# Delta-rule attention and a routed expert layer on one core: keys and queries laid out with rows of zeros between the heads and loaded in one transfer per half turn

## The chip, the cores and the metric

The kernel runs on one core of a Trainium2 chip. The metric is the device time of one execution in microseconds (us). Engines are named as in the profile: PE (TensorE, with its weight loads as PEld), DVE (VectorE), ACT (ScalarE), POOL (GpSimd) and SP (SyncE, which only issues transfers).

## The reference

The first part is a delta rule over 768 steps, for 4 batches and 8 heads of 48 features. Its output, as 3072 rows of 384, goes to one of 8 experts each:

```python
k_n = k / (np.linalg.norm(k, axis=-1, keepdims=True) + 1e-06)
for t in range(S):                                    # S = 768
    kt, vt, bt = (k_n[:, :, t], v[:, :, t], beta[:, :, t, None])
    y[:, :, t] = np.einsum('bhd,bhde->bhe', q[:, :, t], state)
    v_old = np.einsum('bhde,bhd->bhe', state, kt)
    state = state + bt[:, :, :, None] * np.einsum('bhd,bhe->bhde', kt, vt - v_old)
...
logits = x @ w_gate                                   # x: (3072, 384), 8 experts
expert_idx = np.argmax(logits, axis=1)
gate_w = softmax(logits) at expert_idx
for e in range(E):
    y[rows of e] = np.maximum(x[rows of e] @ w1[e], 0.0) @ w2[e]      # F = 1024
return gate_w[:, None] * y
```

## The kernel before

The 768 steps are cut into 12 turns (`NT`) of 64 steps (`C`). The 32 pairs of batch and head are held as 16 slots with two heads each: head half e = 0 lies in partitions 0 to 47 and e = 1 in partitions 64 to 111 (`feat`, L298); partitions 48 to 63 between them belong to no head.

**Keys and queries.** `kqA` is a ring of 6 turns (`RING`), 2048 columns of fp32 for each: 1024 columns of keys (k = 0) and 1024 of queries (k = 1), with the features on partitions. `load_kq(t)` (L348) fills one turn with four transfers of 48 partitions by 1024 columns (192 KB), one for each half turn k and head half e. All are issued by SP, but for the e = 1 keys of turns 0 and 1, which ACT issues. The matrix multiplications with the state, `with_state` (L548), contract over partitions 0 to 111, so partitions 48 to 63 of a slot must hold zeros. They come from memsets on POOL for slots 2 to 5 (L332) and slot 0 (L1086), and for slot 1 from two transfers that copy 16 partitions of slot 5 (L336). `kS` (L560) makes each use of the state wait for the zeroing too.

**A turn.** `scores(t)` (L363) multiplies the keys with the keys and queries of the turn on PE. From turn 2 on it does so in two halves through one pair of banks (BY), and ACT evicts each half with two activations (L309, into `blkA` and `pA`) before the next half can start. `invert(n)` (L418) serves two turns: DVE gets the norms `nt` (L472) and then a triangular inverse of 32 by 32 blocks, whose transposed result `TT` (L517) the two turns use. For n = 0 the diagonal blocks come straight from PSUM (L311 and L309); for later n four small transfers copy them from SBUF to SBUF (`blkA<-blkA`). DVE also masks the query-key scores of each turn (L412). `load_kv(t)` (L521) loads the values `v` and the keys by token `kt`; ACT scales the 16 slots of v by the norms (L530, 16 activations). `turn(t)` (L563) is the recurrence: ACT puts v into PSUM, PE adds the state's part (L554), ACT evicts the residual R, PE applies the inverse (L583), ACT evicts Z, PE goes across the two 32-blocks (L593), then R, the inverse and Z once more, and `kz` (L607) with ACT's copies S gives the next state. `output` (L623) writes the turn's rows to `xs`, `logits` and `route` choose the experts, and `early` and `expert` run the experts' two matrix multiplications (L945, L977). `last_rows` (L910) writes 1.18 MB of zeros into the tail of `xs` from the tile `folds`.

**What sets the order.** Every step is recorded with `P.op`: engine, an assumed cost, what it reads and writes, a rank (`prio`) and an assumed latency of its result (`lat`). `Plan.order` (L88) plays these through and so decides in which order each engine gets its instructions; an engine then runs them in that order and waits where data is missing. The constants `cf` (masks, identity, numbers; 128 rows of 805 fp32) are one transfer issued by ACT (L319). Each load uses one of eight completion counters in turn: from the ninth on, the built program issues a load only after the one eight before it is complete.

Of the kernel before, what the change touches and what calls it, by code (L numbers as in the profile page):

```python
# [18 lines left out]
B, H, S, D = 4, 8, 768, 48  # L19
C = 64  # L20
NT = S // C
FQ = 8
# [11 lines left out]
FAR = 1 << 20  # L34
RING = 6
AHEAD = 5
RUN = 4.5
PAGE, FILL, STALL = 125, 3.8, 0.8
OUT, LOG = 0.9, 0.2
# [153 lines left out]
def _consts():  # L193

    p = np.arange(128)[:, None]
    j = np.arange(128)[None, :]
    rev = np.broadcast_to(E - np.arange(E), (128, E))
    first = np.broadcast_to(np.arange(E), (128, E))  # L200
    closed = first + E * EARLY * (first == 0)
    i = np.arange(32)[None, :]
    q = np.arange(64)[None, :]
    parts = [
        ("rev", rev), ("first", first), ("upper", E * (p < j)), ("ones", np.full((128, 128), E)),
        ("ident", p == j), ("numbers", 128 * np.arange(2 * NT)[None, :] + p + 1), ("along", np.broadcast_to(j, (128, 128))),
        ("later", np.concatenate([p % 64 < q, (p % 64) ^ 32 < q], axis=1)), ("fold", p % 32 == i), ("sums", p % 64 == q),
        ("places", np.broadcast_to(E * (CAP + 128 * np.arange((NL - CAP) // 128)), (128, (NL - CAP) // 128))),
        ("closed", closed),
    ]  # L210
    at, where = 0, {}
    for name, a in parts:
        where[name] = (at, a.shape[1])
        at += a.shape[1]
    return np.concatenate([a for _, a in parts], axis=1).astype(np.float32), where
# [3 lines left out]
def tile_kernel(ctx: ExitStack, tc: tile.TileContext, kq, ktok, vtok, betal, wgk, w1, w2, out):  # L219
    nc = tc.nc  # L220
    P = Plan()
# [8 lines left out]
    fc, where = _consts()  # L230
    cf = pool.tile([128, fc.shape[1]], FP32, name="cf")
# [8 lines left out]
    bl = pool.tile([128, NB, 32], FP32, name="bl")  # L240
    cnt = pool.tile([128, E], FP32, name="cnt")
    kqA = pool.tile([128, RING * 2048], FP32, name="kqA")
    pA = pool.tile([128, RING * 1024], FP32, name="pA")
    blkA = pool.tile([128, 13 * 1024], FP32, name="blkA")
    kts = [pool.tile([128, 2 * FQ, D], FP32, name=f"kt{i}") for i in range(2)]

    vs = [pool.tile([128, FQ, 2, D], FP32, name=f"v{i}") for i in range(2)]
# [14 lines left out]
    def kb(b):  # L262
        return [("bk", b), ("bk", b + 1)]
# [3 lines left out]
        return kqA[:, a : a + 2048].rearrange("p (k s c) -> p k s c", k=2, c=C)  # L267

    def kKQ(t, ks=(0, 1)):
        return [("kqA", t % RING, k, e) for k in ks for e in range(2)]  # L270

    def Pm(t):
        a = (t % RING) * 1024
# [19 lines left out]
    SP = lambda b: max(0.5, b / 220e3)  # L293

    def dma(eng, o, i):
        return lambda: eng.dma_start(out=o, in_=i)

    def feat(e):  # L298
        return slice(64 * e, 64 * e + D)
# [16 lines left out]
    P.op("DVE", 0.1, lambda: nc.vector.memset(tiny[:], 0.0), w=["tiny"], prio=-99)  # L316
    P.op("ACT", 0.2, lambda: nc.scalar.activation(out=tiny[:], in_=tiny[:], func=AF.Copy), w=["tiny"], prio=-45)
    P.op("ACT", 0.5, dma(nc.scalar, bl[:], betal), w=["bl"], prio=-49, lat=2.5)
    P.op("ACT", 0.5, dma(nc.scalar, cf[:], nc.inline_tensor(fc, name="c_f32").ap()), w=["cf"], prio=-48, lat=8.5)  # L319
    P.op("DVE", 0.2, lambda: nc.vector.memset(wg[:], 0.0), w=["wg"], prio=-48)  # L320
    P.op("ACT", 0.5, dma(nc.scalar, wg[:, :, 0:E], wgk), w=["wg"], prio=-40, lat=2.5)
    P.op("DVE", 1.0, lambda: nc.vector.memset(pairs[0][:], 0.0), w=kb(BS), prio=-50)
# [4 lines left out]
        for e in range(2):  # L327
            nc.tensor.matmul(bk[BR + e], lhsT=zeros[:, 0:128], rhs=zeros[:], start=True, stop=True, skip_group_check=True)
    P.op("PE", 1.0, adding, r=["zeros"], w=kb(BR), prio=-95, passes=4, use=2048)

    for i in (2, 3, 4, 5):
        P.op("POOL", 1.85, lambda i=i: nc.gpsimd.memset(kqA[:, 2048 * i : 2048 * i + 2048], 0.0),  # L332
             w=kKQ(i) + [("zero", i)], prio=-60)
    for e in range(2):
        r = slice(64 * e + D, 64 * e + 64)
        P.op("SP", 0.6, dma(nc.sync, kqA[r, 2048:4096], kqA[r, 10240:12288]), r=[("zero", 5)], w=[("zero", 1)],  # L336
             prio=-40, lat=2.5)
    empty = pool.tile([128, E * NL // 128 * 2], FP32, name="empty")


# [7 lines left out]
    def load_kq(t):  # L348
        o = kqA[:, (t % RING) * 2048 : (t % RING) * 2048 + 2048]
        for k in range(2):  # L350
            for e in range(2):
                eng, q = (nc.scalar, "ACT") if t < 2 and e and not k else (nc.sync, "SP")
                c = slice(1024 * k, 1024 * k + 1024)
                P.op(q, 0.9, dma(eng, o[feat(e), c], kq[t, e][:, c]), w=[("kqA", t % RING, k, e)],
                     prio=(t - 100 if not k else t - 60) if t < 2 else t - 7, lat=4.4 if t < 2 and not k else 2.5)

    def products():
        for f in range(FQ):
# [4 lines left out]
    def scores(t):  # L363
# [35 lines left out]
        else:  # L399
            for g in range(2):  # L400
                P.op("PE", 1.1, lambda g=g: run(BY, (0, 1), range(4 * g, 4 * g + 4)), r=kKQ(t), w=kb(BY),
                     prio=t - RUN + 0.01 * g, passes=32, use=770)
                src = pairs[3][:].rearrange("p e (f c) -> p e f c", f=4)
# [3 lines left out]
                    src[:, :, :, 0:C].rearrange("p e f c -> p c e f")),  # L407
                    r=kb(BY), w=[("XY", n % 3, u, g)], prio=t - RUN)
                P.op("ACT", 0.5, copy("ACT", Pm(t)[:, :, 4 * g : 4 * g + 4, :], src[:, :, :, C:]),
                     r=kb(BY), w=[("P", t % RING)], prio=t - RUN)  # L410
        later = const("later").rearrange("p (e c) -> p e c", e=2).unsqueeze(2).to_broadcast([128, 2, FQ, C])
# [108 lines left out]


    def load_kv(t):
        P.op("SP", SP(393216), dma(nc.sync, vs[t % 2][:].rearrange("p f e d -> p (f e d)"), vtok[t]),
             w=[("v", t % 2)] + [("vn", t % 2, i) for i in range(2 * FQ)], prio=t - 3.5, lat=4.0 if t < 2 else None)
        P.op("SP", SP(393216), dma(nc.sync, kts[t % 2][:].rearrange("p f d -> p (f d)"), ktok[t]),
             w=[("kt", t % 2)], prio=t - 3.4, lat=4.0 if t < 2 else None)
        nt, u = nts[t // 2 % 3], t % 2
        for i in range(2 * FQ):
            v = vs[t % 2][:, i % FQ, i // FQ, :]
            P.op("ACT", 0.225, lambda v=v, i=i: nc.scalar.activation(  # L530
                out=v, in_=v, func=AF.Copy, scale=nt[:, 16 * u + i : 16 * u + i + 1]),
                r=[("nt", t // 2 % 3), ("v", t % 2)], w=[("vn", t % 2, i)], prio=t - VP)
# [25 lines left out]
                    )  # L558

    def kS(t):  # L560
        return [("S", t % 2, e) for e in range(2)] + [("zero", t % RING)]

    def turn(t):  # L563

# [485 lines left out]

    for i in range(NT + AHEAD + 1):
        t = i - AHEAD
        for m, g in enumerate(groups):
            if m >= CLOSE and g[-1] == 2 * t - 3:
                route(m, 1)
        if t > 0:
            output(t - 1)
            if 2 * t - 3 == groups[CLOSE][-1]:
                listed(range(CLOSE + 1), BY, LISTS)
                early_rows()  # L1060
            elif t == NT:
                listed([CLOSE + 1], BY, L3)
        if 0 <= t < NT:
            load_kv(t)
            turn(t)
        if t > 0:
            logits(t - 1)
            for m, g in enumerate(groups):
                if g[-1] == 2 * t - 1:
                    route(m, 0)  # L1070
                    if t == NT:
                        route(m, 1)
                        listed([m], BY, L4)
                elif m < CLOSE and g[-1] == 2 * t - 3:
                    route(m, 1)
        if i < NT:
            load_kq(i)
            scores(i)
        if i % 2 == 0 and 2 <= i <= NT:
            invert(i // 2 - 1)  # L1080
            if i == 2:

                for j in range(2):
                    P.op("POOL", 1.4, lambda j=j: nc.gpsimd.memset(Sbs[j][:], 0.0), r=[("nt", 0)],
                         w=[("S", j, e) for e in range(2)], prio=-15)
                P.op("POOL", 1.85, lambda: nc.gpsimd.memset(kqA[:, 0:2048], 0.0), r=[("nt", 0)],  # L1086
                     w=kKQ(0) + [("zero", 0)], prio=0)
                last_rows()
    prepare(1)
    numbered(rows_i[:], lst[:, :, 0], "rows_i", ["lst"], -74)  # L1090
# [39 lines left out]
    with tc.If(flag > 0):  # L1130
# [6 lines left out]
        with tc.For_i(0, E, 1) as ev:  # L1137
            nt = nc.values_load(more_i[0:1, ds(ev, 1)], min_val=0, max_val=NM)
# [37 lines left out]
def _layout(q, k, v, beta, wg, w1):  # L1176


    def split(a):
        return a.reshape(2, 2, 4, 2, NT, C, *a.shape[3:])  # L1180

    def turned(a):
        a = a.reshape(2, 2, 4, 2, NT, 2, 32, *a.shape[3:]).copy()
        a[:, :, :, 1] = a[:, :, :, 1, :, ::-1]
        return a

    sk, sq = turned(k).reshape(2, 2, 4, 2, NT, C, D), split(q)
    kq = np.stack([sk, sq], axis=0)
    kq = kq.transpose(5, 4, 7, 0, 1, 2, 3, 6).reshape(NT, 2, D, 2048)
    tok = lambda a: turned(a).transpose(4, 0, 5, 6, 3, 1, 2, 7).reshape(NT, 128, 2 * FQ * D)  # L1190
    bl = turned(beta).reshape(2, 2, 4, 2, NB, 2, 2, 32)
    bl = bl.transpose(0, 6, 5, 3, 1, 2, 4, 7).reshape(128, NB, 32)

    vt = turned(v).transpose(4, 0, 5, 6, 1, 2, 3, 7).reshape(NT, 128, 2 * FQ * D)
    g = wg.reshape(NK, 128, E).transpose(1, 0, 2)
    return [np.ascontiguousarray(a) for a in (kq, tok(k), vt, bl, g, w1)]


# [21 lines left out]
```

## Time and profile before

| what | value |
|---|---|
| runs shown (4), median, lowest, highest | 530.85, 530.15, 535.84 us |
| the profiled execution: its own time, its span | 528.61 us, 526.8 us |
| granted TensorE clock, mean | 0.954 |
| key and query loads issued by SP, count, size | 46 x 192 KB |
| HBM read, written | 49.67 MB, 11.01 MB |

The profile page shows the span in 40 equal slices of 13.17 us. Its rows for the clock and the transfers are

```profile
PEclk9557999999999999999799999999999999999997
DMA  8995555465433342695353323513632401000000
GB/s 189 221 239 178 147 155 147 123 164 128 109 95 96 122 143 65 209 391 165 124 178 119 111 94 137 180 24 128 197 119 62 146 3 44 3 17 31 0 31 13
```

A digit is the share in tenths: of full clock speed in the first row, of the time in which the 16 DMA engines were busy in the second. The third is what they moved. In slices 1 and 2 (13 to 39 us) the clock is at half speed and the DMA engines are busy 90% or more at 221 and 239 GB/s, while slice 17 reaches 391 GB/s. A line of a timeline reads: start, length, engine, line, operation, output from input, shapes, count, and in brackets the idle time of that engine just before and what ended it. SPq, ACTq and PEq are the issuing queues of these engines.

### The profile page before, as it was taken

The page shows a single profiled execution, that of the slowest core. Times are in us where ns is not written, and L with a number is a line of the kernel's source. Part 1 is how long each engine was busy: PE and PEld are TensorE (multiplying, and loading weights), DVE is VectorE, ACT ScalarE, POOL GpSimd, SP SyncE. Part 2 cuts the span into 40 slices and gives each one's busy share as a digit, 9 for nine tenths or more (in the row PEclk, how much of TensorE's full clock was granted, in tenths as well). Part 3 has the DMA queues.
Part 4 walks back from the last instruction along what each step waited for, and adds up shares of the span by engine and source line. Part 5 has one row for each costly group of instructions (what it writes and reads, how often), then busy time and mean ns, then how long its engine had stood idle before and what let it go on. Part 6 is the DMA issues. An engine that isn't in the chain of part 4 may idle for free. (4 is left out here: it accounts for less than half of the span.)

```text
span 526.8 us, 15767 instructions
## 1 busy us (share of the span) xinstructions
PE 464.3 (88%) x6816; PEld 317.6 (60%) x6817; DVE 242.0 (46%) x957; ACT 191.9 (36%) x453; POOL 85.0 (16%) x91
## 2 busy tenths in 40 slices
PE   6458888788888889997999999999999999999991
PEld 4347677677777678765755555555556555555550
DVE  4997999999899951541303012212030220121110
ACT  5386979798898855300110111010100101100100
POOL 9100000000100011026210221401402302011020
PEclk9557999999999999999799999999999999999997
DMA  8995555465433342695353323513632401000000
GB/s 189 221 239 178 147 155 147 123 164 128 109 95 96 122 143 65 209 391 165 124 178 119 111 94 137 180 24 128 197 119 62 146 3 44 3 17 31 0 31 13
DMA packets 27849, 63.84 MB, mean 121 GB/s; under 512 B 4026, under 2 KB 16220, under 8 KB 27744
## 3 DMA queue, kind: packets, MB, share of 16 engines
q1 hardware_dynamic: 23376, 52.44, 33.7%
q0 software_dynamic: 3584, 9.44, 5.3%
q10 hardware_dynamic: 816, 0.92, 0.8%
q8 instruction: 54, 0.88, 0.7%
q14 instruction: 19, 0.16, 0.1%
HBM read 49.67 MB, written 11.01 MB: 115 GB/s over the span
## 5 line engine op out<-in xcount | busy, mean ns | idle before, releaser
L945 PE MATMUL pair<-kqA,blkA 128*128 128x416 f32 (+2 forms) x288 | 90.5, 472 | 2.9 <-issue 1.8
L977 PE MATMUL pair<-blkA,kqA 128*128 128x384 f32 x240 | 79.0, 488 | 0.0
L951 DVE TENSOR_SCALAR kqA<-pair 128x416 f32<-128x416 f32 (+2 forms) x36 | 19.5, 543 | 126.4 <-PE pair L945 116.9
L945 PEld LDWEIGHTS pair<-kqA,blkA 128*128 128x128 f32 x288 | 54.3, 202 | 35.0 <-issue 31.1
L977 PEld LDWEIGHTS pair<-blkA,kqA 128*128 128x128 f32 x240 | 45.1, 190 | 33.3 <-issue 3.1
L893 POOL DMA_INDIRECT out<-y,rows_i x30 | 28.7, 958 | 199.6 <-DVE y L1038 122.7
L954 ACT ACTIVATE kqA<-pair 128x416 f32<-128x416 f32 (+2 forms) x36 | 17.2, 479 | 115.3 <-PE pair L945 111.6
L968 ACT ACTIVATE y<-pair,lst 128x384 f32<-128x384 f32 x15 | 8.7, 581 | 128.0 <-PE pair L977 111.9
L373 PE MATMUL pair<-kqA 48*64 48x128 f32 (+1 forms) x896 | 37.3, 319 | 18.1 <-ACT pA L309 10.7
L530 ACT ACTIVATE v<-v,nt 128x48 f32<-128x48 f32 x192 | 48.8, 328 | 6.4 <-DMA v<-in_vtok 6.0
L945 PE MATMUL pair<-kqA,pA 128*128 128x416 f32 x144 | 51.0, 513 | 0.0
L977 PE MATMUL pair<-pA,kqA 128*128 128x384 f32 x144 | 47.2, 488 | 0.0
L373 PEld LDWEIGHTS pair<-kqA 48*64 48x64 f32 x896 | 30.0, 176 | 24.5 <-ACT pA L309 11.7
L945 PEld LDWEIGHTS pair<-kqA,pA 128*128 128x128 f32 x144 | 27.1, 190 | 22.6 <-issue 21.6
L977 PEld LDWEIGHTS pair<-pA,kqA 128*128 128x128 f32 x144 | 27.1, 190 | 20.2 <-issue 1.9
L554 PE MATMUL pair<-S,kqA 112*64 112x96 f32 x704 | 34.2, 249 | 4.4 <-ACT S L309 2.8
L886 POOL DMA_INDIRECT kqA<-xs,rows_i x30 | 29.8, 994 | 50.6 <-DVE any_i L1118 27.6
L554 PEld LDWEIGHTS pair<-S,kqA 112*64 112x64 f32 x704 | 29.9, 137 | 7.0 <-issue 2.8
L583 PE MATMUL pair<-R,blkA 32*32 32x48 f32 x1536 | 27.8, 221 | 3.3 <-ACT R L309 2.8
L965 DVE TENSOR_SCALAR y<-pair,lst 128x384 f32<-128x384 f32 x7 | 4.3, 617 | 54.9 <-PE pair L977 54.9
L583 PEld LDWEIGHTS pair<-R,blkA 32*32 32x32 f32 x1536 | 24.6, 145 | 7.4 <-ACT R L309 4.6
L490 DVE TENSOR_TENSOR prod<-blkA 128x16 f32<-128x16 f32 (+7 forms) x96 | 27.8, 289 | 0.0
(136 smaller groups left out, 598.7 us busy)
## 6 DMA issues: line engine op xcount, KB each, us to landing
kqA<-in_kq SPq DMA_DIRECT2D x46, 192.0 KB, 5.0
blkA<-in_w SPq DMA_DIRECT2D x15, 512.0 KB, 5.1
blkA<-in_w SPq DMA_DIRECT2D x10, 768.0 KB, 5.4
v<-in_vtok SPq DMA_DIRECT2D x12, 384.0 KB, 4.3
kt<-in_ktok SPq DMA_DIRECT2D x12, 384.0 KB, 4.4
xs<-x SPq DMA_DIRECT2D x12, 384.0 KB, 4.1
pA<-in_w SPq DMA_DIRECT2D x9, 512.0 KB, 3.5
pA<-in_w SPq DMA_DIRECT2D x6, 768.0 KB, 10.9
```

The lines of the kernel that those rows point to most:

```text
L373: nc.tensor.matmul(bk[bank + e][half(x), i * w : i * w + w].rearrange("p (k c) -> p k c", c=C), lhsT=v[feat(e), 0, x * FQ + f, :], rhs=v[f ...
L490: dve(16 * w, lambda j=j, w=w, pl=pl: nc.vector.tensor_tensor(out=pl, in0=gl[:, 16:32, j : j + 1].to_broadcast([128, 16, w]), in1=u[:, j : ...
L530: P.op("ACT", 0.225, lambda v=v, i=i: nc.scalar.activation(out=v, in_=v, func=AF.Copy, scale=nt[:, 16 * u + i : 16 * u + i + 1]), r=[("nt" ...
L554: nc.tensor.matmul(bk[bank + g][half(x ^ g if first else x), 2 * D * i : 2 * D * i + 2 * D], lhsT=KQ(t)[0 : 64 + D, k, x * FQ + f, :], rhs ...
L583: nc.tensor.matmul(at(BZ, f, e)[quad(q)], lhsT=tt[quad(q), :, 16 * u + 8 * e + f], rhs=R[quad(q), f, e, :], start=True, stop=True, skip_gr ...
L886: nc.gpsimd.indirect_dma_start(out=dst, out_offset=None, in_=xs, in_offset=bass.IndirectOffsetOnAxis(ap=idx, axis=0), bounds_check=N - 1, ...
L893: nc.gpsimd.indirect_dma_start(out=out, out_offset=bass.IndirectOffsetOnAxis(ap=idx, axis=0), in_=src, in_offset=None, bounds_check=N - 1, ...
L945: nc.tensor.matmul(bk[b][:, 0:n], lhsT=a1[:, s, f * 128 : f * 128 + 128], rhs=xT[:, s, :], start=(s == 0), stop=(s == NK - 1))
L951: (lambda f=f, b=b: nc.vector.tensor_scalar(out=hT[:, f, :], in0=bk[b][:, 0:n], scalar1=0.0, scalar2=None, op0=OP.max))
L954: (lambda f=f, b=b: nc.scalar.activation(out=hT[:, f, :], in_=bk[b][:, 0:n], func=AF.Relu)),
L968: (lambda: nc.scalar.activation(out=y[0:n], in_=bk[b][0:n, 0:DM], func=AF.Copy, scale=gate)),
L977: nc.tensor.matmul(bk[b][:, 0:DM], lhsT=hT[:, f, at : at + 128], rhs=a2[:, f, :], start=(f == 0), stop=(f == NF - 1))
```

## The change

The host lays keys and queries out as 112 rows a turn: 48 features of e = 0, 16 rows of zeros, 48 features of e = 1. `load_kq` then fills a half turn with one transfer of 112 partitions, always issued by SP. The memsets and copies that zeroed partitions 48 to 63 go, with the waits for them. The transfer of the constants moves from ACT to SP, with a rank that places it third. The assumed costs and latencies of the loads of keys, queries, `v` and `kt` are set anew, which alters the planned order. In the built program PE's order is the same as before. On DVE the mask of turn 5 stands two small operations earlier. On ACT the first 16 scalings of v stand as 6 and 10 around the eviction of turn 2's second half (before: 1, 11 and 4 around both halves), the Z of turn 0's second inverse follows the last eviction of turn 5's scores instead of standing between its two activations, and one scaling of the third turn's v stands ahead of the first copies S. On SP the transfer of `folds` stands ahead of the third turn's v.

```diff
     def kKQ(t, ks=(0, 1)):
-        return [("kqA", t % RING, k, e) for k in ks for e in range(2)]
+        return [("kqA", t % RING, k) for k in ks]
...
-    P.op("ACT", 0.5, dma(nc.scalar, cf[:], nc.inline_tensor(fc, name="c_f32").ap()), w=["cf"], prio=-48, lat=8.5)
+    P.op("SP", 1.35, dma(nc.sync, cf[:], nc.inline_tensor(fc, name="c_f32").ap()), w=["cf"], prio=-70, lat=4.0)
...
-    for i in (2, 3, 4, 5):
-        P.op("POOL", 1.85, lambda i=i: nc.gpsimd.memset(kqA[:, 2048 * i : 2048 * i + 2048], 0.0),
-             w=kKQ(i) + [("zero", i)], prio=-60)
-    for e in range(2):
-        r = slice(64 * e + D, 64 * e + 64)
-        P.op("SP", 0.6, dma(nc.sync, kqA[r, 2048:4096], kqA[r, 10240:12288]), r=[("zero", 5)], w=[("zero", 1)],
-             prio=-40, lat=2.5)
...
         for k in range(2):
-            for e in range(2):
-                eng, q = (nc.scalar, "ACT") if t < 2 and e and not k else (nc.sync, "SP")
-                c = slice(1024 * k, 1024 * k + 1024)
-                P.op(q, 0.9, dma(eng, o[feat(e), c], kq[t, e][:, c]), w=[("kqA", t % RING, k, e)],
-                     prio=(t - 100 if not k else t - 60) if t < 2 else t - 7, lat=4.4 if t < 2 and not k else 2.5)
+            c = slice(1024 * k, 1024 * k + 1024)
+            P.op("SP", 1.35, dma(nc.sync, o[0 : 64 + D, c], kq[t][:, c]), w=[("kqA", t % RING, k)],
+                 prio=(t - 100 if not k else t - 60) if t < 2 else t - 7, lat=LOAD if t < 2 and not k else 3.0)
...
-        P.op("SP", SP(393216), dma(nc.sync, vs[t % 2][:].rearrange("p f e d -> p (f e d)"), vtok[t]),
-             w=[("v", t % 2)] + [("vn", t % 2, i) for i in range(2 * FQ)], prio=t - 3.5, lat=4.0 if t < 2 else None)
+        P.op("SP", 1.2, dma(nc.sync, vs[t % 2][:].rearrange("p f e d -> p (f e d)"), vtok[t]),
+             w=[("v", t % 2)] + [("vn", t % 2, i) for i in range(2 * FQ)], prio=t - 3.5, lat=8.0 if t < 2 else 3.0)
...
     def kS(t):
-        return [("S", t % 2, e) for e in range(2)] + [("zero", t % RING)]
+        return [("S", t % 2, e) for e in range(2)]
...
-                P.op("POOL", 1.85, lambda: nc.gpsimd.memset(kqA[:, 0:2048], 0.0), r=[("nt", 0)],
-                     w=kKQ(0) + [("zero", 0)], prio=0)
...
+    rows = np.zeros((NT, 64 + D, 2048), np.float32)
+    rows[:, 0:D], rows[:, 64:] = kq[:, 0], kq[:, 1]
```

`LOAD` is 3.6; `kt` is changed as `v` is.

## The prediction

> **What bounds the kernel now.** I read the busy slices first, then the waits of VectorE and ScalarE in the first 80 us, then the timelines around them, then the DMA rate by stage.
>
> From the page:
>
> ```profile
> span 526.8 us, 15767 instructions
> PE 464.3 (88%) x6816; PEld 317.6 (60%) x6817; DVE 242.0 (46%) x957; ACT 191.9 (36%) x453; POOL 85.0 (16%) x91
> ...
> PE   6458888788888889997999999999999999999991
> ...
> DVE  4997999999899951541303012212030220121110
> ```
>
> A slice is 13.17 us. PE is full from slice 15 on (the experts); until then DVE is the busiest engine. The change touches loads that end by slice 10, so it can only move the start, and what it saves there must come through the DVE-bound slices and then push a full PE to the left. The waits of DVE up to 80 us, and of ScalarE between 15 and 30 us (what waited <- for whom, total, times, longest):
>
> ```profile
> DVE blkA L311 <- PE pair L373: 5.9, 1, 5.9
> DVE pA L412 <- ACT pA L309: 3.0, 1, 3.0
> ```
>
> ```profile
> ACT v L530 <- DMA v<-in_vtok: 6.0, 1, 6.0
> ```
>
> So DVE has one hole worth having after its start, 2.95 us, and ScalarE has one of 6.04 us. The timelines of ACT, PE and DVE join them (start, length, what; idle time before it in brackets):
>
> ```profile
> 16.95 1.02 ACT L309 ACTIVATE pA<-pair 128x1024 f32<-128x1024 f32 x1 [2.10 <-PE pair L373]
> 24.02 0.34 ACT L530 ACTIVATE v<-v,nt 128x48 f32<-128x48 f32 x1 [6.04 <-DMA v<-in_vtok]
> 24.26 0.58 ACT L309 ACTIVATE blkA<-pair 128x512 f32<-128x512 f32 x1
> 24.74 0.59 ACT L309 ACTIVATE pA<-pair 128x512 f32<-128x512 f32 x1
> ```
>
> ```profile
> 18.08 2.10 PE L373 MATMUL pair<-kqA 48*64 48x128 f32 x32 [1.19 <-ACT pA L309]
> ```
>
> ```profile
> 50.26 1.23 DVE L412 TENSOR_TENSOR pA<-pA,cf 128x1024 f32<-128x1024 f32 x1 [2.95 <-ACT pA L309]
> ```
>
> The scores of turn 2 are done at 20.18, but their eviction stands behind a scaling of v0 that waits for its load until 24.02. Every later score half follows in a chain PE, ACT, PE (starts 25.38, 28.86, 32.38, 35.84, 39.11), and turn 0's first inverse is behind the 39.11 one in PE's order: it starts at 41.02 though its factor is ready at 37.35 (the transposition of 36.64 plus 0.71). The same chain makes DVE wait at 50.26. Turn 2's inverse needs the second factor (transposition 73.30 to 74.00) and starts at 74.07; from there on the factors are early (101.06 against an inverse at 104.98), so the recurrence on PE and ACT sets the pace. DMA rates by stage (length, clock, DMA share, GB/s):
>
> ```profile
> 14.00:16.00 2.00, 0.50 1.10 209
> 22.50:23.50 1.00, 0.50 1.07 377
> 223.00:227.00 4.00, 1.00 1.03 420
> ```
>
> All three are saturated: 48-partition key loads move 209 GB/s, the 128-partition v/k loads about 377, weights 420.
>
> **The loads.** A pair of 196,608 B transfers becomes one of 458,752 B (112 x 4 KB). No 112-partition transfer is in the trace. Bounds: 209 GB/s (2.20 us) and 420 GB/s (1.09 us), against 1.88 us for the pair now. I take 7/8 of the mid of 367 and 420, 344 GB/s: 112 rows as long as 128, 1.33 us, because the row count is nearer to 128 than to 48. With both halves in flight on two queues (2 to 8 us) the rate is 227 GB/s, little over the 209 of one after the other, so it is not the order of issue that limits these loads. [...]
>
> v0's load ends 4.58 MB into the queue (8 loads 3.67, constants 0.41, betas and gates 0.11, v0 0.39). First bytes come at about 1.9 us; the first matmul at 5.24 against its 393 KB at some 213 GB/s (3.7) gives 1.5 us from bytes to use. So v0 is usable at 1.9+13.3+1.5 = 16.7, or 25.3 at 209 GB/s; ACT wants it at 21.3, met from 256 GB/s up. The ACT hole goes.
>
> **First scores.** Usable at 4.7 and 6.1 (344) or 5.6 and 7.8 (209), against 5.24 and at most 6.9 now; but PE's own zero matmuls end at 5.31. Between a gain of 0.1 and a loss of 0.9; I take 0. The constants, now third on SP, are usable at 1.9+4.2+1.5 = 7.6 (10.3 at 209), needed at 12.53. [...]
>
> **Zeroing.** Five POOL memsets (7.04 + 1.81 us) and two SP copies go. POOL then idles until 36 us either way, and no engine's wait names these memsets. DVE's small operation at 15.32 took 0.37 beside a memset and 0.18 at 47.13 without: DVE gains 0 to 0.2. SP's issues of 0.31 to 0.61 each run beside a full DMA queue: 0.
>
> **The chain, replayed with the new orders.** The changed build keeps PE's order; ACT evicts turn 2's first half before any scaling, then scales 6, evicts, scales 10. Turn 2's eviction starts at 20.2 instead of 24.26; second half on PE 21.4 (-4.0), evicted by 24.45; third half 24.55. Now 10 scalings (2.25), the copy into PSUM (0.81) and R (0.85) follow where 4 scalings did: third eviction at 28.3 instead of 31.24, the rest -2.9. Turn 0's inverse at 38.1 instead of 41.02; the factor (37.2 to 37.35) no longer binds nor waits.
>
> Three edits in ACT's order then cost. Z of turn 0 now follows the last eviction of turn 5 instead of preceding it: +0.6 (one 0.59 activation). One scaling of the next v0 now stands ahead of the state copy S and needs the second norms; behind it wait S and all of turn 1. DVE makes those norms after its mask of turn 5: mask at 46.7 (the eviction ends at 46.6), two 0.2 us steps, reciprocal, transposition: 48.7; ACT then scales until 49.2, S could have started at 48.5: +0.7. Bounds 0 (norms early) and 1.2. One scaling fewer in turn 1: -0.25. Turn 1 and turn 2's inverse: -2.9 + 0.6 + 0.7 - 0.25 = -1.9. DVE: its 0.40 us wait for copies and the 2.95 us shrink to some 0.4, so its factor comes 3.1 earlier (74.0 to 70.9) and does not bind. From turn 2 on nothing else differs, and the later waits name PE, ACT and DVE, which all move; so the profiled execution falls from its own 528.61 to 526.7. The runs shown have the median 530.85, 2.2 above it; I take the same difference off: **528.9**.
>
> **Rivals.**
> - *Slower: 112 partitions move at the 48-partition rate.* The zeros are 0.92 MB more for 14 loads up to turn 6, and the built order puts the 1.18 MB of folds ahead of the next v0 and of the four block copies that DVE's second inversion needs. That queue is 10.1 MB. At 344 GB/s it drains at 31.3, before the copies are issued (32.3 to 34.7); landing takes 3.4 after the last (37.7 to 41.1 now), so 38.1 against a need at 40.5. It decides when the queue drains after 37.1, below 287 GB/s. At 209: drained at 50.2, copies at 53.6, DVE 13.1 late, factor at 84.0 instead of 74.0: 540.9. Against it: 128-partition rows at 377 to 420.
> - *No change: the clock.* PE's granted clock rises from 0.50 to 1.00 between 44 and 46 us. If that stays at its instant while the work moves left, one score half costs 1.99 instead of 1.10 and one inverse 1.51 instead of 1.13: +1.3, leaving -0.6, 530.2.
> - *Faster: the added waits cost nothing.* Then DVE's factor binds, -3.1 to -3.5: 527.5.
> - *The change doesn't do it*: v0 still late, between 209 and 256 GB/s; that is inside the slower one.
>
> **How the numbers follow.** The forecast (-1.3 to -2.5) 0.42, faster 0.20, no change 0.18, slower 0.13, 0.07 for a start that I mis-sized. These are mostly smaller than 1%, 5.3 us, which I take as what a measurement of this kernel can tell from no change. Range: down to 526.0 (DVE floor, start earlier by the 0.9 that I bounded), up to 532.2, which takes in the no-change case, a start 0.9 late and the beginning of the slower rival; left out are its far end and gains over 4.8. Faster by over 1%: 0.06; slower by over 1%: 0.09, two thirds of the slower rival; within: 0.85.
>
> **What would show it.** No ACT wait for v0, or under 1 us; turn 2's second half near 21.4; turn 0's inverse near 38.1; the wait of DVE's turn-5 mask under 1 us; a wait of ACT on DVE ahead of S near 49; turn 2's inverse near 72.2 and the same stages from there. DMA at 300 GB/s or more in 5 to 20 us. I am wrong if key loads stay near 209, if DVE waits for block copies at 40, or if the lead at turn 2 is lost or grows before the experts.

## The result, and the profile after

The changed kernel takes 534.79 us (median of 48 runs, 529.74 to 541.52) against 531.95 us for the kernel before beside it (74 runs, 528.11 to 538.33): a ratio of 1.0042, with an interval of 1.0028 to 1.0056. The ratio is of fast executions alone, without the few in a slower state, so it is not the quotient of these medians (1.0053). The changed kernel is slower by 0.4%, 2.2 us; forecast was a gain of 2.0 us, in a range up to 532.2. The profiled execution took 531.49 us against 528.61. Chips differ by more than that (the kernel before has medians of 525.78 to 531.95 on those used here), so kernels are compared by their ratio to the kernel before on the same chip.

From the page of the changed kernel:

```profile
span 529.7 us, 15712 instructions
...
PEclk8558799999999988999999999999999999999996
DMA  8994365364323431497363333503631500000000
GB/s 211 262 309 126 88 183 164 106 195 134 105 92 95 130 113 48 135 377 253 125 219 119 94 109 136 169 28 134 196 111 47 167 3 31 15 17 31 0 31 14
...
kqA<-in_kq SPq DMA_DIRECT2D x24, 448.0 KB, 8.6
```

55 instructions fewer; the loads are 24 where they were 48. The clock row is lower than before in slice 4 (7, was 9) and in slices 14 and 15 (8, were 9: 185 to 212 us). These last are far from any load that makes PE wait. The rates while keys arrive, by windows of 2 us (length, busy time and count of PE, PEld, DVE, ACT, POOL, then clock, DMA share, GB/s):

```profile
12.00:14.00 2.00, 1.34 (x49) 1.34 (x52) 1.90 (x5) 1.73 (x4) 0.00 (x0) 0.50 1.10 237
14.00:16.00 2.00, 0.86 (x34) 0.67 (x32) 1.69 (x10) 1.02 (x1) 0.00 (x0) 0.50 1.03 236
16.00:18.00 2.00, 2.00 (x64) 1.87 (x60) 1.86 (x8) 0.00 (x0) 0.00 (x0) 0.50 1.02 234
18.00:20.00 2.00, 0.87 (x19) 0.81 (x20) 1.97 (x16) 1.02 (x1) 0.00 (x0) 0.50 1.02 257
```

At 236 GB/s, 458,752 B take 1.94 us: a half turn with its zeros takes as long as the pair without them (1.88). The waits of DVE and of ACT up to 80 us:

```profile
DVE blkA L428 <- DMA blkA<-blkA: 2.2, 1, 2.2
DVE pA L403 <- ACT pA L310: 1.2, 1, 1.2
```

```profile
ACT v L521 <- DVE nt L463: 3.4, 1, 3.4
...
```

The load of v0 is no longer among the long ones (0.68 instead of 6.04). In its place are the block copies, which stand behind the longer queue, and the norms, which DVE makes after them. Timelines of DVE, ACT and PE:

```profile
43.65 0.71 DVE L428 STREAM_TRANSPOSE blkA<-blkA 128x512 f32<-128x512 f32 x1 [2.22 <-DMA blkA<-blkA]
...
49.30 1.22 DVE L403 TENSOR_TENSOR pA<-pA,cf 128x1024 f32<-128x1024 f32 x1
...
51.15 0.15 DVE L463 STREAM_TRANSPOSE nt<-rt 128x32 f32<-128x32 f32 x1
```

```profile
51.34 0.33 ACT L521 ACTIVATE v<-v,nt 128x48 f32<-128x48 f32 x1 [3.38 <-DVE nt L463]
51.58 1.60 ACT L310 ACTIVATE S<-pair 64x768 f32<-64x768 f32 x2
```

```profile
53.33 2.83 PE L545 MATMUL pair<-S,kqA 112*64 112x96 f32 x32 [3.45 <-ACT S L310]
56.09 1.99 PE L364 MATMUL pair<-kqA 48*64 48x128 f32 x32
58.01 1.50 PE L574 MATMUL pair<-R,blkA 32*32 32x48 f32 x64
```

The copies end 2.2 us after DVE wants them, so the mask of turn 5 runs at 49.30 and the norms are there at 51.3. One scaling of 0.33 us that needs them holds the state copy S, and with it PE, for 3.4 us; from 54 to 59 us PE then works at half clock (0.50 granted; the product with the state 2.83 instead of 1.54).

The second loss is late. First the kernel before, then the changed one, both PE timelines after turn 9's first inverse (178.13 and 179.48):

```profile
180.20 1.13 PE L593 MATMUL pair<-Z,blkA 32*32 32x48 f32 x64
181.26 0.39 PE L678 MATMUL pair<-cf,lgT 64*128 64x8 f32 x4
```

```profile
181.55 1.11 PE L584 MATMUL pair<-Z,blkA 32*32 32x48 f32 x60
184.60 0.32 PE L584 MATMUL pair<-Z,blkA 32*32 32x48 f32 x4 [1.94 <-issue]
184.85 0.39 PE L669 MATMUL pair<-cf,lgT 64*128 64x8 f32 x4
185.17 0.71 PE L1110 MATMUL pair<-cf 128*128 128x128 f32 x4
185.88 1.48 PE L574 MATMUL pair<-R,blkA 32*32 32x48 f32 x64
```

The same 64 matmuls run through in the first; in the second PE stops after 60 of them for 1.94 us, waiting for nothing but "issue". No data is late and no other engine is named. Starts of the first inverse of some turns, in us:

| kernel | turn 0 | turn 1 | turn 2 | turn 9 | turn 11 | turn 9 to 11 |
|---|---|---|---|---|---|---|
| before | 41.02 | 55.91 | 74.07 | 178.13 | 207.07 | 28.94 |
| changed | 38.99 | 58.01 | 75.36 | 179.48 | 212.89 | 33.41 |

So 1.3 us are lost by turn 2, and 4.5 between turns 9 and 11. Of these 5.8 us the profiled pair shows 2.9 at the end: before's execution had a stretch at a clock of 0.66 (250 to 260 us, among the experts' products) that the other did not have. One profile is one execution: in a second one of the changed kernel (h0 below) turn 2 is 0.8 us ahead of the kernel before, and of the 3.2 us lost by turn 11 only 0.9 fall between turns 9 and 11.

### The profile page after: what moved, and what is told of

It reads as the page before. It is cut to its first block, busy times and chain, and to the rows that moved or that the text cites. A ratio compares the mean times of both kernels' runs of the same rounds, so it can differ in the third digit from the quotient of the medians.

```text
span 529.7 us, 15712 instructions
## 1 busy us (share of the span) xinstructions
PE 464.1 (88%) x6816; PEld 317.6 (60%) x6817; DVE 241.9 (46%) x957; ACT 191.8 (36%) x453; POOL 76.2 (14%) x86
## 5 line engine op out<-in xcount | busy, mean ns | idle before, releaser
L936 PE MATMUL pair<-kqA,blkA 128*128 128x416 f32 (+2 forms) x288 | 87.5, 458 | 2.9 <-issue 2.5
L936 PEld LDWEIGHTS pair<-kqA,blkA 128*128 128x128 f32 x288 | 51.3, 190 | 35.0 <-issue 31.8
L545 PEld LDWEIGHTS pair<-S,kqA 112*64 112x64 f32 x704 | 31.1, 141 | 8.6 <-issue 4.3
```

The source lines that it names most:

```text
L545: nc.tensor.matmul(bk[bank + g][half(x ^ g if first else x), 2 * D * i : 2 * D * i + 2 * D], lhsT=KQ(t)[0 : 64 + D, k, x * FQ + f, :], rhs ...
L936: nc.tensor.matmul(bk[b][:, 0:n], lhsT=a1[:, s, f * 128 : f * 128 + 128], rhs=xT[:, s, :], start=(s == 0), stop=(s == NK - 1))
```

## The experiments

Twelve kernels, on three chips, each timed beside the kernel before except the first. The first four expectations set theories on the first turns against each other: RATE (the loads of 112 partitions are slow in themselves) with CROWD (slow by the traffic beside them), ORDER (the order on ScalarE) and CLOCK.

**e1_rates.** Nothing but loads, all else left out: eight half turns in each of seven forms, one after the other.

```diff
+stages = [pair48, pair48_two_queues, rows 0:112, rows 0:128, 0:64 and 64:112, rows 0:96, rows 0:64]
```

> This kernel leaves out the whole computation; it only loads rows of 4 KB from HBM, eight half turns a stage, all stages parted by a VectorE copy: pairs of 48 partitions on SP; the same pairs on SP and ACT; 112 partitions; 128 partitions; 64 and 48 partitions; 96 partitions; 64 partitions. Theory RATE (a 112-partition load moves no faster than a pair of 48s, for a reason that lies in the load itself): pairs about 209 GB/s (1.88 us each), 112 partitions 235 to 255 GB/s (1.8 to 1.95 us), 128 partitions 380 GB/s or more (1.4 us or less). Rival CROWD (in the changed kernel other transfers or a start-up effect slowed the loads): 112 partitions alone reach 330 GB/s or more (1.4 us or less). If 128 partitions stay under 260 GB/s as well, both fall, and what slows these loads is how the source lies in HBM.

The windows lie inside the first six stages, in that order (length, DVE, POOL, clock, DMA share, GB/s):

```profile
12.00:22.00 10.00, 0.00 (x0) 0.00 (x0) 1.00 1.03 222
28.00:38.00 10.00, 0.00 (x0) 0.00 (x0) 1.00 1.00 229
44.00:54.00 10.00, 0.00 (x0) 0.00 (x0) 1.00 0.98 280
60.00:68.00 8.00, 0.00 (x0) 0.00 (x0) 1.00 0.97 338
76.00:86.00 10.00, 0.00 (x0) 0.00 (x0) 1.00 1.03 245
93.00:102.00 9.00, 0.00 (x0) 0.00 (x0) 1.00 1.00 248
```

112 partitions move 280 GB/s alone, not the 344 of the forecast, and between what RATE (235 to 255) and CROWD (330 or more) expected: 1.64 us a half turn against 1.77 for the pair (393,216 B at 222). 128 partitions move 338, less than the 380 that RATE expected, and need 1.55 us although they carry 14% more. A second queue brings 3%. All stages keep the DMA engines fully busy (0.97 to 1.03), so it is their speed by form that differs. The loads are slow in themselves, and slower still in the kernel (236); why they lose there, while 128 partitions gain (380, below), is not shown.

**a2_scale_behind_state.** One instruction moved.

```diff
+seq.remove(mark["scale", 2, 0])
+seq.insert(seq.index(mark["S", 0, 1]) + 1, mark["scale", 2, 0])
```

> The changed kernel with one instruction moved: the scaling of the third turn's first slot of v goes behind the two state copies S of turn 0 on ACT; all other instructions stand as they did. Theory ORDER (the lead of 2.0 us that turn 0 has is lost in the 3.4 us that ACT waits for the second norms): S at about 48.2 to 49 instead of 51.58, turn 1's first inverse at 53.5 to 54.7 instead of 58.01, no half-clock spell at 54 to 59 us, turn 2's inverse at 73.5 (its factor) instead of 75.36: 1.9 us less than the changed kernel, so within 0.5 us of the kernel before. Theory CLOCK (what decides is the half-clock spells near 186 and 201 us, which come or go by themselves): same early milestones, but the time stays within 0.7 us of the changed kernel.

1.0017 (0.9977 to 1.0056). Its PE timeline:

```profile
53.92 1.10 PE L364 MATMUL pair<-kqA 48*64 48x128 f32 x32
54.95 1.14 PE L576 MATMUL pair<-R,blkA 32*32 32x48 f32 x64
...
67.08 1.03 PE L632 MATMUL pair<-Z,pA 64*64 64x48 f32 x55 [1.80 <-issue]
...
75.99 1.13 PE L576 MATMUL pair<-R,blkA 32*32 32x48 f32 x64
```

The wait for the norms falls from 3.4 to 0.6, and turn 1's inverse comes 3.06 us earlier. Turn 2's does not: DVE's factor is no earlier (its transposition ends at 73.72, in the changed kernel at 73.48), and PE has issue stalls of 1.07 and 1.80 in between. So the wait is real, but turn 2's inverse comes 2.5 us after the 73.5 that ORDER expected, and the time is told apart neither from the changed kernel's nor from the kernel before's.

**b1_rows128.** Sixteen more rows of zeros, loads of 128 partitions; every order stays.

```diff
-rows = np.zeros((NT, 64 + D, 2048), np.float32)
+rows = np.zeros((NT, 128, 2048), np.float32)
...
-dma(nc.sync, o[0 : 64 + D, c], kq[t][:, c])
+dma(nc.sync, o[:, c], kq[t][:, c])
```

> The changed kernel with 128 rows a turn (16 more rows of zeros at the end) and loads of 128 partitions; every engine's order is unchanged. Theory RATE: loads at 350 GB/s or more, first scores at 5.3 and 6.9 or earlier instead of 6.03 and 7.92, no ACT wait for v0, block copies landed before VectorE wants them (no wait instead of 2.2 us), norms near 48.3, ACT's wait for them under 0.8, turn 2's inverse at 71 to 72.5 instead of 75.36: 3 to 4 us less than the changed kernel, 0.7 to 1.7 less than the kernel before. Theory ORDER alone: the 3.4 us wait stays near 2.5 and the gain is under 1.5 us. If the rate of 128 partitions is no better, it is 0 to 2 us slower than the changed kernel, as 14% more bytes are moved.

0.9978 (0.9948 to 1.0009). The window of 8 to 20 us:

```profile
8.00:20.00 12.00, 5.27 (x165) 4.54 (x168) 10.61 (x46) 7.32 (x14) 0.00 (x0) 0.70 1.00 380
```

```profile
47.61 0.33 ACT L521 ACTIVATE v<-v,nt 128x48 f32<-128x48 f32 x1 [2.95 <-DVE nt L463]
```

The rate is 380 GB/s, and the waits for v0 and for the block copies are gone. ACT's wait for the norms is not: it is 2.95 us, where RATE expected under 0.8 and ORDER about 2.5. Turn 2's inverse is at 70.67, 3.4 us ahead of the kernel before. By turn 9 it is 2.8 ahead; by turn 11, with stalls of 1.91 and 1.12 us at the same two places as in the changed kernel, it is 0.9 behind.

**c2_rows128_scale.** Both edits.

> Loads of 128 partitions and the scaling behind the state copies. RATE and ORDER together: no wait for v0, block copies or norms; turn 1's inverse near 52.5, turn 2's inverse bound by its factor at 70.5 to 71.5: 3.5 to 4.5 us less than the changed kernel, 1 to 2 less than the kernel before. If ORDER is the whole cause, equal to the run with the moved scaling alone within 0.7 us; if RATE is, equal to the run with 128 rows alone within 0.7 us.

1.0006 (0.997 to 1.0042). Turn 1 at 52.38, turn 2 at 70.42, turn 9 at 175.87, turn 11 at 207.00, with a stall of 1.92 us after turn 9. All kernels built from the changed one had lost 31 to 33 us there where the kernel before needs 28.9. PE's order is the same in all of them. What the change does remove from PE's stream is waits: the trace counts 51 semaphore instructions on PE instead of 64, while matmuls and weight loads stay at 6816 each. That gave a new theory, FETCH: the losses lie at the boundaries between the blocks in which PE's instructions arrive. The plan of both kernels already reckons with such blocks: `Plan.order` counts pages of 125 matmuls (`PAGE`) and gives each 3.8 us to come in (`FILL`). But it counts matmuls alone, not the waits between them.

What it rests on: one queue of the trace (q8) has 54 transfers of kind "instruction" with 0.88 MB, so 16 KB each. And six issue stalls of the kernel before fall after 2002, 2258, 2513, 2640, 2895 and 3151 matmuls, that is 256, 255, 127, 255 and 256 apart; with a weight load for each, 128 matmuls are 256 instructions. Counting all of PE's records (matmuls, weight loads, waits) makes it exact: in the thirteen profiles of the whole kernel, all 82 issue stalls of 0.5 us or more between 40 and 215 us come after a number of instructions that leaves 193 or 194 when divided by 256. Thirteen instructions fewer move such boundaries six or seven matmuls further on in the same code.

**h0_copy.** The changed kernel as it is, as a measure for the next three.

> The changed kernel itself, beside the kernel before and the next three on one chip, as their common measure. Both theories: 1.004 (1.002 to 1.006) times the time of the kernel before. Turn 9's first inverse to turn 11's takes 33 us (32 to 34; the kernel before 28.9), with an issue stall of TensorE of 1.9 us about 6 us into it.

1.0051 (1.0021 to 1.0081). The stall is there, on another chip:

```profile
185.57 0.31 PE L584 MATMUL pair<-Z,blkA 32*32 32x48 f32 x4 [1.92 <-issue]
```

```profile
49.67 0.34 ACT L521 ACTIVATE v<-v,nt 128x48 f32<-128x48 f32 x1 [3.23 <-DVE nt L463]
```

Turn 9 to turn 11 took 29.80 us, not the 32 to 34 expected: no half clock followed the stall here. In the first profile it did (0.51 granted over 186 to 188 us: 1.48 for the inverse at 185.88, and 2.07 for eight filler matmuls that take 1.16 here). Here slow stretches came earlier: at 92.93 the product with the state takes 2.83 instead of 1.54, right behind a boundary stall of 0.96, and at 131.01 `kz` takes 1.53 instead of 0.94. From turn 2 to turn 9 this execution took 107.2 us, the first profile and the kernel before 104.1. The block copies kept DVE waiting 0.5 us instead of 2.2, yet ACT stood 3.23 us for the norms, as the second line shows.

**h7_shift** and **b7_rows128_shift.** Tiny matmuls at PE's start, in the changed kernel and in the one with 128 rows. Each was issued as two, so 28 instructions instead of the 14 meant. They begin a new sum in a bank into which the recurrence adds R, so the values that follow are others; the instructions are not, but these two times carry less weight.

```diff
             nc.tensor.matmul(bk[BR + e], lhsT=zeros[:, 0:128], rhs=zeros[:], start=True, ...)
+        for _ in range(7):
+            nc.tensor.matmul(bk[BR + 1][:, 0:8], lhsT=zeros[:, 0:128], rhs=zeros[:, 0:8], start=True, ...)
```

> The changed kernel with seven tiny matmuls of zeros more at TensorE's start (128x8 outputs, before the first keys have come): 14 instructions, as many as TensorE's stream has lost by turn 9; the order on every engine stays. FETCH theory: TensorE's instructions come in blocks of 256 (16 KB each, 54 of them), and with fewer waits in the stream the block boundaries fall elsewhere in it; with the boundaries back, the stall of 1.9 us at the product Z<-blkA of turn 9 is below 0.3, the gap of 7.5 us between two instruction fetches there is below 6.5, turn 9's first inverse to turn 11's takes 29 to 31 us, and the run is 0.3 to 0.8% faster than the copy of the changed kernel. START theory (all of the loss is made in the first three turns by the late loads and the wait for the norms, and what comes later only carries it or is chance): the stall is chance, the stretch stays at 31 to 34 us, and the time agrees with the copy within 0.2%.

> The layout of 128 rows (key loads on all 128 partitions, 16 rows of zeros more) and the seven tiny matmuls together. FETCH theory: the 4 us that 128 rows gain up to turn 9 are kept through turn 11: turn 9's first inverse to turn 11's 29 to 31 us, span 519 or less, 0.992 to 0.996 of the kernel before and 0.8 to 1.2% faster than the copy of the changed kernel. START theory: as 128 rows alone, 0.995 to 1.001 of the kernel before.

0.9963 (0.9931 to 0.9995) and 0.9939 (0.9905 to 0.9973). No issue stall at that place in either, and 29.18 and 28.77 us from turn 9 to turn 11. h7 and h0 ran on the same chip, and their intervals do not touch. But most of h7's lead lies ahead of that place: turn 9 is at 176.25, in h0 at 180.47. In the second the tiny matmuls (2.99 us) hold the first scores until 8.03, so the lead of 128 rows is not in it (turn 9 at 179.66).

**d2_const_act.** The constants back on ACT's queue, behind the betas and the gate's weights (in the kernel before they stood ahead of these weights and of the load of ACT's table).

```diff
-    P.op("SP", 1.35, dma(nc.sync, cf[:], ...), w=["cf"], prio=-70, lat=4.0)
+    P.op("SP", 1.35, dma(nc.scalar, cf[:], ...), w=["cf"], prio=-70, lat=4.0)
```

> The changed kernel with the constants back on ScalarE's queue, at their place in ScalarE's order behind the betas and the gate's weights; every other instruction stays. Both theories: this part is worth little. The second key load is freed of 0.4 MB ahead of it on SyncE's queue, but the two queues share the engines (229 GB/s together against 222 alone for pairs of 48): first scores 0 to 1 us earlier, scaled v of turn 0 and the block copies within 0.5 us of the copy's, time within 0.2% of the copy of the changed kernel. If the constants were what delays turn 0, turn 0's inverse would come 1 us or more earlier and the time fall by 0.2 to 0.4%.

1.0075 (1.0045 to 1.0106), not clear of the copy's interval. But what it does early was expected by neither theory:

```profile
DVE blkA L428 <- DMA blkA<-blkA: 3.5, 1, 3.5
...
ACT ents L310 <- DMA cf<-c_f: 6.4, 1, 6.4
```

Issued at 3.44 us beside SP's full queue, the constants land 17.0 us later; ACT stands 6.4 us for them, and turn 0's inverse is at 44.70 instead of 38.70. So a place behind the key loads on the other queue is a bad one; whether the constants' old place would have been is not tried.

**i4_tiny, k4_rows128_tiny, m4_rows128_scale_tiny.** The same idea cleanly: four tiny matmuls (16 instructions) behind the first scores, where PE waits anyway, added into columns that only fillers use; in the changed kernel, with 128 rows, and with 128 rows and the moved scaling.

```diff
+            def first():
+                run(b, (0,), range(FQ))
+                for _ in range(4 * t):
+                    nc.tensor.matmul(pairs[1][:, 1, DM : DM + 8], lhsT=zeros[:, 0:128], rhs=zeros[:, 0:8],
+                                     start=False, stop=True, skip_group_check=True)
```

> The changed kernel with four tiny matmuls of zeros (each issued as two, with two weight loads: 16 instructions), now behind the first scores, where TensorE waits 3 us for ScalarE, added into columns that only filler matmuls use. FETCH theory: the block boundaries lie within an instruction or two of where they lay in the kernel before at turns 9 and 10; no issue stall of more than 0.5 us at the product Z<-blkA of turn 9, no gap of more than 6.5 us between two instruction fetches there, turn 9's first inverse to turn 11's 28.5 to 30.5 us, and 0.998 to 1.002 of the kernel before (what is left of the loss is turn 1's wait for the norms and the block copies). START theory: the stall of 1.9 us stays and 1.003 to 1.006 of the kernel before.

> 128 rows and the same four tiny matmuls. FETCH theory: no stall of 1.9 us, the stretch from turn 9 to turn 11 28.5 to 30.5 us, turn 11's first inverse at 203.5 to 206 (128 rows alone 208.0), 0.992 to 0.996 of the kernel before. START theory: stretch and time as 128 rows alone (32.6 us, 0.995 to 1.001).

> 128 rows, turn 2's one v-scaling behind turn 0's second state, and the four tiny matmuls. FETCH theory: turn 1's inverse 1 us earlier than with 128 rows and the tiny matmuls alone, of which turn 2's inverse keeps 0 to 0.3 (as in the pair without the tiny matmuls), so the same time within 0.2%: 0.991 to 0.996 of the kernel before. START theory, by which the norms' wait is what costs: 0.4 to 0.6% faster than 128 rows with the tiny matmuls.

**j4_before_less.** The opposite: the kernel before, with four filler matmuls (16 instructions) taken out of the first turns.

```diff
+        for i in [i for i in seq if i >= len(P.ops)][:4]:
+            seq.remove(i)
```

> The kernel before, without its first four filler matmuls (16 instructions less on TensorE by turn 2; the filler writes to columns that nothing reads): the block boundaries move to within an instruction or two of where the changed kernel has them at turn 9, and nothing else of the change is in it. FETCH theory: the kernel before now has the stall too: 1.5 to 2.2 us of issue at the product Z<-blkA of turn 9 with a gap of 7 to 7.6 us between two instruction fetches, turn 9's first inverse to turn 11's 31 to 33.5 us (28.9 with the fillers), and 1.002 to 1.007 of the kernel before. START theory: no such stall, time within 0.2% of the kernel before.

PE timelines, first of i4, then of j4, at the place of the stall:

```profile
181.56 1.13 PE L589 MATMUL pair<-Z,blkA 32*32 32x48 f32 x64
182.63 0.39 PE L674 MATMUL pair<-cf,lgT 64*128 64x8 f32 x4
```

```profile
182.44 1.13 PE L593 MATMUL pair<-Z,blkA 32*32 32x48 f32 x62
185.22 0.31 PE L593 MATMUL pair<-Z,blkA 32*32 32x48 f32 x2 [1.65 <-issue]
```

With 16 instructions more the changed kernel runs through; with 16 fewer the kernel before stops, two matmuls from where the changed one did. j4 lost more than the 1.002 to 1.007 expected, and not all of it at that place: 1.2 us by turn 2, 4.2 between turns 9 and 11. The fillers that it leaves out ran from 48.78 us on. PE's products are slower than the kernel before's on both sides of that place: scores 1.56 instead of 1.10 at 46.70, the inverse 1.51 instead of 1.13 at 48.19, the masked scores' product 1.92 instead of 1.11 at 51.95 (the kernel before has a clock of 1.00 over 47 to 54 us). Whether the missing work has a part in the first loss was not tried apart. Windows of 180 to 212 us of i4 and j4:

```profile
180.00:212.00 32.00, 29.79 (x984) 25.93 (x980) 16.65 (x90) 18.61 (x35) 3.60 (x3) 1.00 0.34 105
```

```profile
180.00:212.00 32.00, 27.80 (x817) 24.08 (x818) 17.04 (x91) 16.08 (x32) 3.38 (x3) 0.89 0.27 91
```

The granted clock is 1.00 without the stall and 0.89 with it, as in the kernel before (1.00) and the changed one (0.89); h0 has the stall and kept 1.00. The instruction fetches themselves, their starts as worked out from the trace's DMA records (us from the span's start):

```
before   165.46  169.48  173.35  177.84  181.88  185.82  191.65
changed  167.21  171.48  174.79  182.26  185.74  190.70  196.83
i4       167.39  171.39  174.72  179.19  183.25  186.92  192.69
j4       167.81  171.83  175.70  182.96  186.35  191.30  197.31
```

The changed kernel and i4 run the same code at the same time up to turn 9's inverse (179.48 and 179.49). i4 has asked for its next 16 KB before that inverse starts, the changed kernel 3.1 us later. In both stalling kernels PE resumes 2.3 us after the fetch starts (182.26 to 184.60, 182.96 to 185.22).

| kernel | ratio to the kernel before | turn 2 | turn 9 | turn 11 | turn 9 to 11 |
|---|---|---|---|---|---|
| h0, the changed kernel | 1.0051 (1.0021 to 1.0081) | 73.24 | 180.47 | 210.27 | 29.80 |
| i4, changed + 16 instructions | 1.0012 (0.9984 to 1.0040) | 74.75 | 179.49 | 208.13 | 28.64 |
| b1, 128 rows | 0.9978 (0.9948 to 1.0009) | 70.67 | 175.36 | 208.00 | 32.64 |
| k4, 128 rows + 16 | 0.9930 (0.9896 to 0.9964) | 70.35 | 177.09 | 207.29 | 30.20 |
| c2, 128 rows, scaling | 1.0006 (0.9970 to 1.0042) | 70.42 | 175.87 | 207.00 | 31.13 |
| m4, 128 rows, scaling + 16 | 0.9904 (0.9870 to 0.9939) | 71.46 | 177.29 | 206.24 | 28.95 |
| j4, before - 16 | 1.0110 (1.0062 to 1.0157) | 75.25 | 180.38 | 213.54 | 33.16 |

In every pair the 16 instructions are worth 0.4 to 1.0%. The two kernels of a pair ran on different chips, so only their ratios compare; the intervals of the first two pairs touch, those of c2 and m4 do not, and j4 lies clear of 1. That the stall goes with the boundary is shown in both directions. How much of the time is this one stall is not: part of what is gained by turn 11 can be lost again, as from 212 us on the clock is 0.97 in i4 and in the kernel before, with its stretch of 0.66 among the experts' products, and 0.98 to 0.99 in h0, the changed kernel and j4, which have the stall. Turn 11 of k4 and m4 came later than the 203.5 to 206 expected of k4: both reach turn 9 about 1.5 us later than their pairs, with other stalls on the way (1.47 at 121.00 in k4, 1.50 at 49.74 in m4). So moving the boundaries helps at one place and costs at others. m4 is faster than both kernels. That its moved scaling adds to k4 is not shown: their intervals overlap, and turn 1 came 0.7 us later than in k4 (53.24 and 52.51), not the expected 1 us earlier.

## Why the prediction was wrong

- **The step that failed: "From turn 2 on nothing else differs".** It compared the order of PE's work and found it the same, and took the waits that the change removes for free. They are instructions. Thirteen fewer move every later block boundary, and both profiles of the changed kernel show PE standing 1.9 us at one place after turn 9 where the kernel before runs through. With the low clock behind it (0.51 over 186 to 188 us, 0.50 over 200 to 202), turns 9 to 11 cost 4.5 us in the first profile, where the step had 0; in h0 they cost 0.9, and turns 2 to 9 cost 3.2. With the shift undone (i4) the changed kernel is at 1.0012, not told apart from the kernel before. That interval touches the changed kernel's own (1.0028 to 1.0056). Two runs do better: h7 against h0 on one chip, 0.9963 and 1.0051 with intervals apart, and the other direction, j4, where 16 instructions fewer cost the kernel before 1.1%. That shifting the boundaries changes the time is shown; how the 0.4% divides among the places is not.
- **The load at 344 GB/s, 1.33 us, was mis-sized.** Measured: 236 in the kernel (1.94 us), 280 alone. This goes with the missing gain: in i4, where the late loss is gone, the time is still 0.5% above the forecast (1.0012 against 528.9/530.85, 0.9963). At 128 rows the rate is 380 and 524,288 B take 1.38 us, nearly what the forecast had for 112: there, with the late loss undone as well (k4, on i4's chip), 0.9930, and the intervals do not touch. The row count looked near to 128, but 112 (280 alone) behaves more like 96 (248) than like 128 (338). Two smaller readings were loose: 227 against 209, "little over", is a gain of 9%, where alone a second queue brought 3% (229 against 222); and the 367 in the mid is the row of 22.5 to 23.0 us, not the 377 that was shown.
- **The ACT hole on v0 goes.** Right, 6.04 to 0.68: even 236 GB/s, under the 256 named as the limit, leaves little, as the scores ahead of v0 were late too. v0 was used from 23.01, where the sum had 16.7. Turn 0's inverse came at 38.99 (forecast 38.1, before 41.02), and the mask of turn 5 no longer waits.
- **First scores, priced 0 between -0.1 and +0.9.** They started at 6.03 instead of 5.24: +0.8, inside the bounds, at the end that belongs to the slow rate.
- **The scaling ahead of S, +0.7 (0 to 1.2), took 3.4 us.** Place and mechanism were right, the size was not. The sum had DVE's mask at 46.7 and the norms at 48.7; in the first profile DVE stood 2.2 us for the block copies, and they came at 49.30 and 51.3. The copies alone do not make the wait, though: it is 3.23 us in h0 beside a copies' wait of 0.5, and 2.95 with 128 rows, where DVE does not wait for them, because turn 0's Z, ACT's last work ahead of it, comes earlier too (43.85 instead of 47.15). Turn 2's inverse was at 75.36, in h0 at 73.24, forecast 72.2. Yet by a2 this wait has cover: without it turn 2 is no earlier.
- **The slower rival** had the right cause of the first turns (112 partitions near the 48-partition rate, the queue drained late, the block copies late) and its bound of 287 GB/s holds: at 234 to 257 the queue drained at about 41 us (37.1 was the limit) and DVE waited 2.2. Its price of 12 us stood for 209 GB/s. That the kernel ends above the range was missed because the late loss was in no case.
- **The clock rival** asked only whether full clock still comes at 44 to 46 us. It came earlier, within 42 to 44 us (mean 0.83; the kernel before 0.50), so the price of 1.3 did not fall due. The clock did cost, but behind stalls: at 54 to 59 us (0.50) and in stretches between 186 and 204 (mean 0.81).
- **The constants** on SP have no term in the sum, which has them usable at 7.6 against a need at 12.53; no wait of the changed kernel names them: right.

## What to carry to other kernels

In e1 a load's rate went by the partitions it wrote, and not in proportion (248 GB/s for 96, 280 for 112, 338 for 128): measure the very shape, or fill all 128 partitions; more bytes were less time here (1.55 us a half turn against 1.64). Thirteen waits fewer on PE, busy 88% of the span, shifted its instruction blocks by six or seven matmuls under the later code: after an edit that removes waits or other small instructions, look for idle time that ends with "issue", and test with a handful of empty instructions before crediting or blaming the edit. Such a shift moved the time of these kernels by 0.4 to 1.1%, so a gain of half a per cent says little before it has been tried at another alignment.

## What the runs showed of the hardware

- PE's instructions came in transfers of 16 KB (54 in the changed kernel and in the one before), and all 82 issue stalls counted stand at one place in a block of 256. At the two stalls whose fetches are listed, in the changed kernel and j4, PE resumed 2.3 us after the fetch started (182.26 and 182.96). The stall after turn 9 is in seven of the thirteen profiles and absent in six, as the position of the boundary goes; it lasts 1.65 (j4) to 1.94 us (the changed kernel). In six of the seven the next inverse takes 1.28 to 1.51 us instead of the kernel before's 1.13, in h0 1.13.
- Why the next fetch starts 3.1 us later with the boundary a few matmuls later (182.26 in the changed kernel, 179.19 in i4) is not shown. A wait for ScalarE lies near it (0.49 us before the inverse, in the kernel before as in the changed one, i4 and j4); whether it has a part was not tried.
- Loads on the first 64 + 48 partitions in two transfers moved 245 GB/s (e1), in one of 112 with the gap filled 280 (e1), of 128 338 alone (e1) and 380 in the kernel (b1, 8 to 20 us), where other 128-partition loads are mixed in. 112 partitions, 280 alone, moved 234 to 257 in the kernel (12 to 20 us).
